# Transposes of the early blocks' exponentials: from the scores' banks into the bank of the small products

## Chip, cores and metric

The kernel runs on one core of a Trainium2 chip. The metric is the device time of one execution in microseconds; a lower time is better. The engines are named as in the profile: PE is the matrix engine (PEld its weight loads, PEldq and PEq its queue), DVE the vector engine, ACT the scalar engine, POOL GpSimd, SP the queue that starts most transfers.

## What is computed

Three parts follow each other: attention over a window of 128 positions with a bias that falls with distance, a dense layer pair, and a mixture of eight experts of which each token uses one. The shapes are 4 batches, 8 heads, 576 positions, 64 numbers a head, so 2304 tokens of 512 numbers.

```python
scores = q @ k.T / sqrt(64);  scores = where(0 <= i - j < 128, scores + bias, -1e9)
x = softmax(scores) @ v                       # attention, to (2304, 512)
h = x @ w_in;  x = (h - tanh(h)) @ w_out      # 512 -> 2048 -> 512
e = argmax(norm(x) @ norm(emb).T / tau)       # one expert of 8 a token
out = gate * (relu(x @ w1[e]) @ w2[e])        # 512 -> 1024 -> 512
```

## The kernel before

The 2304 tokens are 18 blocks of 128. A block's attention is cut into four quarters of two heads each, `jj` 0 and 1 (`quarter`, called with `a = 4 * b + ...`). The first four blocks (`early`, `b < 4`, quarters 0 to 15) take another way than the rest: their scores are made from float32 q and k (L456), and their exponentials are turned by TensorE, where the later blocks write them as two float16 halves and have a transfer turn them (L513).

One early quarter is this chain, for `jj` 0 and 1 each: `scores` on PE (L456, 128 queries by 128 keys for the first block, by 256 for the others); `soft` on DVE (L484), which adds the bias in place and takes the row extreme; `exp` on ACT (L498) into the SBUF tile `p32`, which has two places that quarters use in turn; `tr_pe` on PE (L518), one transpose of 128x128 for each 128 keys; `tr_out` on ACT or DVE (L524), the copy of the turned exponentials into `pt`; and then, for both heads, `pv_f` on PE (L535), the product with the values. After every second quarter DVE divides by the sums (L553, L554, L572), and after a whole block `x_out` turns the block's 512 columns on PE (L633) and splits them into a high and a low part (L645 on ACT, L646 on DVE).

PSUM has eight banks of 2 KiB a partition. Two of them belong to the scores, one for each `jj`. Before the change each holds a tile of 512 float32 numbers a partition in two halves, the scores in half 0 and the turned exponentials in half 1:

```python
self.scores = [self.psA.tile([128, 2, 2, 128], F32, ...) for n in range(2)]
sc = self.scores[jj][:, 0]      # scores()
t = self.scores[jj][:, 1]       # tr_pe(), tr_out()
```

The waits between engines are placed from the tiles that instructions touch, in the order in which the instructions are issued. One more bank, `misc` (`Builder.misc`), serves the small products in turn: the turned embedding of the experts (L269), the turned blocks of `x_out`, and later those of the routing. Its content is held from the product to the last read of it.

The order of all instructions on all engines is made by a list scheduler (`Plan`). Each step is added with its engines and their assumed costs, a due time, and the keys that it reads and writes; `take="misc"` and `free="misc"` mark the first and the last user of the shared bank, and a step that takes it isn't placed while another holds it. Of the steps that are ready, `Plan.order` places the one that can start first, at equal starts the one with the lower due time, and where a step may go to several engines the one that ends it first. Each engine then works strictly in that order. An early quarter's due times rise by half a unit a quarter.

At the same time as the early blocks, the weights `w_in` and `w_out`, which arrive as 64-bit integers, are turned into pairs of float32 parts on ACT (L307, L313, L325), DVE (L309, L313, L328, L331) and POOL or DVE (L317). The dense layer pair starts between the quarters as soon as its first weights and blocks are ready (L686 into the bank `h`, L691 to L703 between, L710 into `acc`).

Of the kernel before, what the change touches and what calls it, by code (L numbers as in the profile page):

```python
# [10 lines left out]
F32 = mybir.dt.float32  # L11
# [151 lines left out]
class Builder:  # L163
# [15 lines left out]
    def setup(self):  # L179
        nc, i = self.nc, self.i  # L180
        self.cst = self.pool("cst", bufs=1)
        self.rt = self.pool("rt", bufs=1)
        self.m1 = self.pool("m1", bufs=2)
        self.xTs = [self.m1.tile([128, XR, KD, 128], F32R, name=f"xT{n}", bufs=1) for n in range(2)]
        self.wp = self.pool("wp", bufs=1)
        self.at = self.pool("at", bufs=2, side="right")
        self.psA = self.pool("psA", bufs=1, space=PSUM)

        self.con = self.cst.tile([128, 129 + E + E + NB], F32, name="con")
        c = iter(np.cumsum([0, 128, E, E, NB, 1]).tolist())  # L190
        c0 = next(c)
        cut = []
        for c1 in c:
            cut.append(self.con[:, c0:c1])
            c0 = c1
        self.ident, self.em8, self.ebase, self.tokid, self.tau = cut
        self.tri = self.cst.tile([128, 128], BF16, name="tri")
        self.ones = self.cst.tile([128, 128], BF16, name="ones")
        self.half = self.cst.tile([128, 1], F32, name="half")
        self.NOV = (NT - CAP + 127) // 128  # L200
        self.thr = self.cst.tile([1, E, self.NOV], F32, name="thr")
        self.cnt = self.cst.tile([128, E], F32, name="cnt")
        self.big = self.cst.tile([128, E], F32, name="big")
        self.cap = self.cst.tile([128, E], F32, name="cap")
        self.gap = self.cst.tile([128, E], F32, name="gap")
        self.ids = self.cst.tile([1, 3 * E], I32, name="ids")
        self.nt = self.cst.tile([1, 2 * E + 1], I32, name="nt")
        self.enT = self.cst.tile([128, KD, E], F32, name="enT")
        self.wst = self.rt.tile([128, 2 * ROW], F32, tag="x2row", name="wst", bufs=1)
        self.wf = [self.wst[:, 0:512], self.wst[:, 512:1024], self.rt.tile([128, 512], F32, tag="xt", name="wst2", bufs=1)]  # L210
        self.wf += [self.at.tile([128, 512], F32, name=f"wf{n}", bufs=1) for n in range(NWF - 3)]
        self.bias = self.at.tile([128, H, 2 * 128], BF16, name="bias", bufs=1)
        self.khl = self.at.tile([128, 2, H, 128], F32R, name="khl", bufs=1)
        self.vt = self.at.tile([128, 2, H, 3 * D], BF16, name="vt", bufs=1)
        self.scores = [self.psA.tile([128, 2, 2, 128], F32, tag=f"sc{n}", name=f"sc{n}") for n in range(2)]
        self.cum = self.rt.tile([128, E], BF16, name="cum")
        self.oh = self.rt.tile([128, 2, E], BF16, name="oh")

# [217 lines left out]
    def quarter(self, P, a, due):  # L436

        nc = self.nc
        b, qd = divmod(a, 4)
        hf, qq = divmod(qd, 2)  # L440
        s, n = b % 2, (2 * b + hf) % 2
        one = b in NOPRE
        W = 128 if one else 256
        v = {"sc": [None, None], "mx": [None, None]}
        pb = a % 2 if a < NPX else 0
# [2 lines left out]
        sk = (a // 2) % 2  # L448

        def scores(jj):  # L450
            sc = v["sc"][jj] = self.scores[jj][:, 0]
            j = qq + 2 * jj
            hp, p0 = hf * 4 + j, 64 * jj
            if early:
                x = slice(1, 2) if one else slice(0, 2)
                nc.tensor.matmul(sc[:, 0:W // 128, :], lhsT=self.qf[b // 2][p0:p0 + 64, b % 2, hf * 2 + qq, :],  # L456
                                 rhs=self.kf[max(b, 1)][p0:p0 + 64, x, hf * 2 + qq, :], start=True, stop=True)
                return
            q = self.qst[n]
            sl = s if one else slice(0, 2)  # L460
            for m in range(2):
                nc.tensor.matmul(sc[:, sl, :], lhsT=q[:, m, j, :], rhs=self.khl[:, sl, hp, :], start=(m == 0),  # L462
                                 stop=(m == 1))
# [48 lines left out]
            v["pt"] = self.at.tile([128, 8, 128], F16, tag=f"pt{a % 2}", name="pt", bufs=1)  # L512
            nc.sync.dma_start_transpose(out=v["pt"][:, 0:4 * W // 128, :], in_=v["ph"][:, 0:4 * W])  # L513

        def tr_pe(jj):
            t = self.scores[jj][:, 1]
            for x in range(W // 128):
                nc.tensor.transpose(t[:, x, :], v["p32"][:, jj * W + x * 128:jj * W + (x + 1) * 128], self.ident)  # L518

        def tr_out(e, jj):  # L520
            if jj == 0:
                v["pt"] = self.at.tile([128, 512], F32, tag=f"pt{a % 2}", name="ptf", bufs=1)
            t = self.scores[jj][:, 1].rearrange("p s t -> p (s t)")
            (nc.scalar.copy if e == "ACT" else nc.vector.tensor_copy)(  # L524
                out=v["pt"][:, jj * W:(jj + 1) * W], in_=t[:, 0:W])

        def pv_f(e):
            KB = W // 128
# [52 lines left out]
        for jj in range(2):  # L581
            if early:
                P.add({"PE": 0.45 if one else 0.65}, lambda e, jj=jj: scores(jj), due,
                      r=["at", ("qf", b)] + [("kf", max(b, 1), x) for x in ([1] if one else [0, 1])], w=[("sc", jj)])
            else:
                P.add({"PE": 0.11 if one else 0.22}, lambda e, jj=jj: scores(jj), due,
                      r=["at"] + ks + [("kl", x, hf) for x in kv] + q, w=[("sc", jj)])
        for jj in range(2):
            P.add({"DVE": ttr}, lambda e, jj=jj: soft(jj), due, r=["at", ("bias", qd * 2 + jj)],
                  w=[("sc", jj), ("mx", jj, a % 2)])  # L590
        for jj in range(2):
            P.add({"ACT": 0.57 if one else 0.67}, lambda e, jj=jj: exp(jj), due,
                  r=["at", ("sc", jj), ("mx", jj, a % 2)], w=[("p32", pb, jj), ("sm", sk, qq, jj)])
        sm = [("sm", sk, x, y) for x in range(2) for y in range(2)]
        half = [("xr", 2 * hf), ("xr", 2 * hf + 1)]
        if early:
            for jj in range(2):
                P.add({"PE": 0.28 if one else 0.5}, lambda e, jj=jj: tr_pe(jj), due, r=["at", "con", ("p32", pb, jj)],
                      w=[("tp", jj)])
            for jj in range(2):  # L600
                P.add({"ACT": 0.3, "DVE": 0.29} if one else {"ACT": 0.38, "DVE": 0.42}, lambda e, jj=jj: tr_out(e, jj),
                      due, r=["at", ("tp", jj)], w=[("pt", a % 2, 1)] if jj else [("pt", a % 2), ("pt", a % 2, 1)])
            P.add({"PE": 0.85 if one else 1.65}, pv_f, due,
                  r=["at", ("pt", a % 2), ("pt", a % 2, 1)] + [("vf", x) for x in ([b] if one else [b - 1, b])], w=[("o", qq)] if qq else ["o", ("o", 0), ("o", 1)])
            if qq:
                P.add({"DVE": 0.5}, recip, due, r=["at"], w=sm)
                P.add({"DVE": 0.4}, mul, due, r=["at", "o", ("o", 0), ("o", 1)] + sm, w=half if hf else [("xr", m) for m in range(4)])
            return
        P.add({"ACT": 0.25, "DVE": 0.2} if one else {"ACT": 0.47, "DVE": 0.34}, s_hi, due, r=["at", ("p32", pb, 0), ("p32", pb, 1)],
              w=[("ph", a % 2)])  # L610
        P.add({"POOL": 0.6, "DVE": 0.33} if one else {"POOL": 1.02, "DVE": 0.6}, s_lo, due,
              r=["at", ("p32", pb, 0), ("p32", pb, 1), ("ph", a % 2)], w=[("ph", a % 2, 1)])
        P.add({"SP": 0.5 if one else 0.9}, tr, due, r=["at", ("ph", a % 2), ("ph", a % 2, 1)], w=[("pt", a % 2)])
        P.add({"PE": 0.27 if one else 0.53}, pv, due,
              r=["at", ("pt", a % 2)] + [("vt", x, hf, m) for x in kv for m in range(3)], w=["o"])
# [802 lines left out]
```

## Time and profile before

| what | value |
|---|---|
| time, median of 3 runs (lowest to highest) | 847.39 us (847.25 to 847.75) |
| the profiled execution: time / span of its instructions | 849.56 us / 847.8 us |
| PE busy / weight loads busy, share of the span | 96% / 85% |
| DVE, ACT, POOL busy, share of the span | 67%, 52%, 30% |
| the early quarters' transposes (L518) on PE | 56, first at 7.3 us, last at 84.5 us |
| their copies (L524) | 32: 26 on ACT, 6 on DVE |

The span runs from the first to the last instruction of the profiled execution. A busy share is a mean over stages that have different limits. Before about 143 us the kernel prepares weights and the early blocks; after that PE runs nearly without a break to the end.

### The profile page before, as it was taken

How to read it: one execution, taken by the hardware profiler on the slowest of the kernel's cores; microseconds unless marked ns; L12 is line 12 of the kernel's file. 1: busy time of each engine (PE TensorE's matmuls, PEld its weight loads, DVE VectorE, ACT ScalarE, POOL GpSimd, SP SyncE). 2: the span in 40 equal slices, each digit the busy share in tenths (PEclk: the TensorE clock that was granted, in tenths of full speed). 3: DMA queues.
4: the chain of work that ended last, by engine and by line, in shares of the span. 5: the costliest groups of instructions: out<-in, count | busy, mean ns of one | idle time of the engine just before them, and what ended most of it. 6: DMA issues, size and time to landing. Idle time of an engine off the chain costs nothing.

```text
span 847.8 us, 15246 instructions
## 1 busy us (share of the span) xinstructions
PE 816.7 (96%) x5244; PEld 721.2 (85%) x5244; DVE 565.5 (67%) x1500; ACT 441.6 (52%) x997; POOL 252.1 (30%) x246
## 2 busy tenths in 40 slices
PE   6999999999999999999999999999999999999995
PEld 4677878988888899988998998989889899998994
DVE  4658999987778577777776775576366656666230
ACT  3759876665555355555554543464255545545120
POOL 1424676554424233324242240021110210111011
PEclk9999999999999999999999999999999999999998
DMA  8973325945334234433434312365266656555000
GB/s 299 334 268 121 109 94 160 270 107 130 96 82 135 40 82 106 87 87 91 99 83 102 80 41 48 125 212 162 84 198 216 216 166 189 193 163 174 20 27 30
DMA packets 109464, 112.88 MB, mean 133 GB/s; under 512 B 62901, under 2 KB 75189, under 8 KB 109248
## 3 DMA queue, kind: packets, MB, share of 16 engines
q1 hardware_dynamic: 106240, 102.35, 42.2%
q0 software_dynamic: 3136, 9.46, 3.0%
q8 instruction: 43, 0.70, 0.4%
q14 instruction: 45, 0.37, 0.1%
HBM read 87.12 MB, written 17.48 MB: 123 GB/s over the span
## 4 chain that ended last, share of the span: by engine, by line
PE 71%; DVE 11%; DMA 7%; issue 6%; ACT 2%; SPq 2%; POOL 1%; POOLq 0%; DVEq 0%; ACTq 0%
PE h L686 19%; PE acc L710 17%; PE he L1014 9%; PE y L1049 8%; PE o L546 3%; DMA pt<-ph 3%; PE sc L456 3%; PE sc L462 2%; DMA out<-yo,ix 2%; DVE wst L331 2%; PE y L1045 2%; PE misc L785 2%; PE of L535 2%; DVE rawo L328 1%; PE sc L518 1%
## 5 line engine op out<-in xcount | busy, mean ns | idle before, releaser
L686 PE MATMUL h<-xT,wi 128*128 128x256 f32 x1728 | 228.8, 287 | 0.0
L686 PEld LDWEIGHTS h<-xT,wi 128*128 128x128 f32 x1728 | 219.4, 193 | 6.4 <-issue 2.6
L710 PE MATMUL acc<-wo,gh 128*128 128x512 f32 x576 | 183.9, 400 | 0.0
L710 PE MATMUL acc<-wo,gl 128*128 128x512 f32 x288 | 112.9, 392 | 2.0 <-DVE gl L703 2.0
L710 PEld LDWEIGHTS acc<-wo,gh 128*128 128x128 f32 x576 | 99.7, 189 | 15.1 <-issue 0.7
L691 ACT ACTIVATE t<-h 128x512 f32<-128x512 f32 x72 | 43.1, 599 | 100.3 <-PE h L686 95.3
L1049 PE MATMUL y<-eo,ge 128*128 128x512 f32 x336 | 88.5, 399 | 0.0
L484 DVE CUSTOM_DVE_ANT_0 sc<-sc,bias 128x256 f32<-128x256 f32 (+1 forms) x144 | 52.7, 372 | 46.3 <-PE sc L462 29.4
L498 ACT ACTIVATE p<-sc,mx 128x256 f32<-128x256 f32 (+1 forms) x128 | 59.3, 464 | 34.1 <-DVE mx L484 26.0
L1074 POOL DMA_INDIRECT out<-yo,ix x24 | 23.4, 975 | 176.2 <-PE y L1045 61.0
L1049 PEld LDWEIGHTS y<-eo,ge 128*128 128x128 f32 x336 | 60.0, 188 | 9.7
L710 PEld LDWEIGHTS acc<-wo,gl 128*128 128x128 f32 x288 | 54.1, 188 | 15.1 <-DVE gl L703 2.9
L508 POOL TENSOR_TENSOR ph<-p,ph 128x512 f16<-128x512 f32 (+1 forms) x38 | 46.1, 1214 | 69.3 <-ACT ph L503 26.0
L703 DVE TENSOR_TENSOR gl<-t,gh 128x512 fp32r<-128x512 f32 x72 | 63.0, 876 | 4.6 <-ACT gh L699 4.4
L948 DVE TENSOR_TENSOR eo<-est,eo 128x512 fp32r<-128x512 f32 x60 | 45.0, 752 | 30.4 <-ACT eo L944 29.4
L1036 DVE SCALAR_TENSOR_TENSOR ge<-he,ge 128x256 fp32r<-128x256 f32 x104 | 29.9, 325 | 51.9 <-ACT ge L1030 51.9
L694 DVE TENSOR_TENSOR t<-h,t 128x512 f32<-128x512 f32 x72 | 49.5, 687 | 19.0 <-ACT t L691 19.0
L944 ACT CAST eo<-est 128x512 fp32r<-128x512 f32 x64 | 39.7, 620 | 40.1 <-PE y L1045 21.5
L1014 PE MATMUL he<-xT,ei 128*128 128x320 f32 x384 | 60.4, 309 | 0.0
L1014 PEld LDWEIGHTS he<-xT,ei 128*128 128x128 f32 x384 | 58.3, 188 | 2.3
L1030 ACT ACTIVATE ge<-he 128x320 fp32r<-128x320 f32 (+1 forms) x56 | 24.1, 430 | 67.5 <-PE he L1014 61.7
L1014 PE MATMUL he<-xA,ei 128*128 128x320 f32 (+1 forms) x384 | 59.0, 302 | 0.0
(181 smaller groups left out, 1425.6 us busy)
## 6 DMA issues: line engine op xcount, KB each, us to landing
est<-in_w SPq DMA_DIRECT2D x128, 256.0 KB, 2.9
rawi<-in_w_in SPq DMA_DIRECT2D x16, 512.0 KB, 6.6
rawo<-in_w_out SPq DMA_DIRECT2D x16, 512.0 KB, 7.3
stk<-in_k SPq DMA_DIRECT2D x30, 256.0 KB, 2.7
stq<-in_q SPq DMA_DIRECT2D x28, 256.0 KB, 2.8
bucket<-in_c_pad SPq DMA_DIRECT2D x8, 771.0 KB, 5.8
xe<-bucket SPq DMA_DIRECT2D x17, 257.0 KB, 3.5
vst<-in_v SPq DMA_DIRECT2D x30, 128.0 KB, 2.4
```

Of the source, the lines that this page charges most:

```text
L484: nc.vector.tensor_tensor_reduce(out=x, in0=x, in1=self.bias[:, h, c0:c1], scale=-0.125, scalar=mx[:, 1:2] if m else 3.0e38, op0=ALU.add, ...
L498: nc.scalar.activation(out=v["p32"][:, jj * W:(jj + 1) * W], in_=x, func=AF.Exp, scale=-1.0, bias=v["mx"][jj][:, 0:1], accum_out=self.sums ...
L508: self.eng(e).tensor_tensor(out=ph[:, 2 * W:4 * W], in0=v["p32"][:, 0:2 * W], in1=ph[:, 0:2 * W], op=ALU.subtract)
L686: nc.tensor.matmul(h3(v["h"], f2), lhsT=w[:, a, k, :], rhs=xT[c][:, :, k, :], start=(k == 0 and n == 0), stop=(k == KD - 1 and n == 2))
L691: nc.scalar.activation(out=v["t"], in_=v["h"].rearrange("p a b -> p (a b)"), func=AF.Tanh)
L694: nc.vector.tensor_tensor(out=v["t"], in0=v["h"].rearrange("p a b -> p (a b)"), in1=v["t"], op=ALU.subtract)
L703: self.eng(e).tensor_tensor(out=v["gl"], in0=v["t"], in1=v["gh"].bitcast(F32), op=ALU.subtract)
L710: nc.tensor.matmul(self.acc[g, t], lhsT=v[a][:, c0:c0 + 128], rhs=self.w["o", fs[f2]][:, c, :], start=(first and f2 == 0 and n == 0), stop ...
L944: nc.scalar.copy(out=t[:, 0, :], in_=v["x"])
L948: self.eng(eng).tensor_tensor(out=t[:, 1, :], in0=v["x"], in1=t[:, 0, :].bitcast(F32), op=ALU.subtract)
L1014: nc.tensor.matmul(h[:, 0:N], lhsT=w[:, a, c0:c0 + 128], rhs=xT()[b][:, k, 0:N], start=(k == 0 and n == 0), stop=(k == KD - 1 and n == 2))
L1049: nc.tensor.matmul(y[t], lhsT=gt(f, a)[:, (t - ts[0]) * 128:(t - ts[0] + 1) * 128], rhs=self.w["o", f0 + f][:, b, :], start=(f == 0 and n ...
```

## The change

In the early quarters the transposes of both heads go into one tile from the shared bank `misc`: four of 128x128 (two in the first block) are issued in one step, and one copy of 512 columns (256 in the first block) takes them out, where before each head had its own transposes in the second half of its scores' bank and its own copy. The tiles of the scores keep only the scores. For the scheduler the two transposing steps (0.5 each, 0.28 in the first block) become one (1.0, 0.6) that needs both heads' exponentials and takes `misc`; the two copies (0.38 on ACT or 0.42 on DVE) become one (0.6 or 0.69) that frees `misc`.

```diff
--- before.py
+++ after.py
@@ -212,7 +212,7 @@
         self.bias = self.at.tile([128, H, 2 * 128], BF16, name="bias", bufs=1)
         self.khl = self.at.tile([128, 2, H, 128], F32R, name="khl", bufs=1)
         self.vt = self.at.tile([128, 2, H, 3 * D], BF16, name="vt", bufs=1)
-        self.scores = [self.psA.tile([128, 2, 2, 128], F32, tag=f"sc{n}", name=f"sc{n}") for n in range(2)]
+        self.scores = [self.psA.tile([128, 2, 128], F32, tag=f"sc{n}", name=f"sc{n}") for n in range(2)]
         self.cum = self.rt.tile([128, E], BF16, name="cum")
         self.oh = self.rt.tile([128, 2, E], BF16, name="oh")
 
@@ -448,7 +448,7 @@
         sk = (a // 2) % 2
 
         def scores(jj):
-            sc = v["sc"][jj] = self.scores[jj][:, 0]
+            sc = v["sc"][jj] = self.scores[jj]
             j = qq + 2 * jj
             hp, p0 = hf * 4 + j, 64 * jj
             if early:
@@ -512,17 +512,15 @@
             v["pt"] = self.at.tile([128, 8, 128], F16, tag=f"pt{a % 2}", name="pt", bufs=1)
             nc.sync.dma_start_transpose(out=v["pt"][:, 0:4 * W // 128, :], in_=v["ph"][:, 0:4 * W])
 
-        def tr_pe(jj):
-            t = self.scores[jj][:, 1]
-            for x in range(W // 128):
-                nc.tensor.transpose(t[:, x, :], v["p32"][:, jj * W + x * 128:jj * W + (x + 1) * 128], self.ident)
-
-        def tr_out(e, jj):
-            if jj == 0:
-                v["pt"] = self.at.tile([128, 512], F32, tag=f"pt{a % 2}", name="ptf", bufs=1)
-            t = self.scores[jj][:, 1].rearrange("p s t -> p (s t)")
-            (nc.scalar.copy if e == "ACT" else nc.vector.tensor_copy)(
-                out=v["pt"][:, jj * W:(jj + 1) * W], in_=t[:, 0:W])
+        def tr_pe(e):
+            v["tp"] = self.misc()
+            for x in range(2 * W // 128):
+                c = slice(x * 128, (x + 1) * 128)
+                nc.tensor.transpose(v["tp"][:, c], v["p32"][:, c], self.ident)
+
+        def tr_out(e):
+            v["pt"] = self.at.tile([128, 512], F32, tag=f"pt{a % 2}", name="ptf", bufs=1)
+            (nc.scalar.copy if e == "ACT" else nc.vector.tensor_copy)(out=v["pt"][:, 0:2 * W], in_=v["tp"][:, 0:2 * W])
 
         def pv_f(e):
             KB = W // 128
@@ -594,14 +592,12 @@
         sm = [("sm", sk, x, y) for x in range(2) for y in range(2)]
         half = [("xr", 2 * hf), ("xr", 2 * hf + 1)]
         if early:
-            for jj in range(2):
-                P.add({"PE": 0.28 if one else 0.5}, lambda e, jj=jj: tr_pe(jj), due, r=["at", "con", ("p32", pb, jj)],
-                      w=[("tp", jj)])
-            for jj in range(2):
-                P.add({"ACT": 0.3, "DVE": 0.29} if one else {"ACT": 0.38, "DVE": 0.42}, lambda e, jj=jj: tr_out(e, jj),
-                      due, r=["at", ("tp", jj)], w=[("pt", a % 2, 1)] if jj else [("pt", a % 2), ("pt", a % 2, 1)])
+            P.add({"PE": 0.6 if one else 1.0}, tr_pe, due, r=["at", "con", ("p32", pb, 0), ("p32", pb, 1)], w=[("tp", a)],
+                  take="misc")
+            P.add({"ACT": 0.4, "DVE": 0.42} if one else {"ACT": 0.6, "DVE": 0.69}, tr_out, due, r=["at", ("tp", a)],
+                  w=[("pt", a % 2)], free="misc")
             P.add({"PE": 0.85 if one else 1.65}, pv_f, due,
-                  r=["at", ("pt", a % 2), ("pt", a % 2, 1)] + [("vf", x) for x in ([b] if one else [b - 1, b])], w=[("o", qq)] if qq else ["o", ("o", 0), ("o", 1)])
+                  r=["at", ("pt", a % 2)] + [("vf", x) for x in ([b] if one else [b - 1, b])], w=[("o", qq)] if qq else ["o", ("o", 0), ("o", 1)])
             if qq:
                 P.add({"DVE": 0.5}, recip, due, r=["at"], w=sm)
                 P.add({"DVE": 0.4}, mul, due, r=["at", "o", ("o", 0), ("o", 1)] + sm, w=half if hf else [("xr", m) for m in range(4)])
```

## Rows read from the trace of the kernel before

**Rows 1.** The page, part 1: busy time of PE and of its weight loads.
```profile
PE 816.7 (96%) x5244; PEld 721.2 (85%) x5244; DVE 565.5 (67%) x1500; ACT 441.6 (52%) x997; POOL 252.1 (30%) x246
```

**Rows 2.** Stretches: length, busy time and instructions by engine, granted clock, DMA share, GB/s.
```profile
10.00:66.00 56.00, 55.00 (x189) 39.45 (x188) 33.14 (x95) 34.90 (x96) 15.37 (x14) 1.00 0.89 314
66.00:100.00 34.00, 30.90 (x200) 24.97 (x200) 31.88 (x56) 29.47 (x67) 19.18 (x12) 1.00 0.37 119
100.00:143.00 43.00, 39.88 (x256) 35.28 (x256) 42.14 (x55) 31.83 (x62) 32.50 (x23) 1.00 0.30 93
```

**Rows 3.** Waits of the first 100 us: total us, times, longest us.
```profile
ACT ptf L524 <- PE sc L456: 16.1, 14, 2.5
...
DVE sc L484 <- ACT ptf L524: 13.3, 14, 2.4
...
PE sc L518 <- ACT p L498: 2.0, 4, 1.0
...
PE misc L633 <- DVE xr L572: 1.7, 1, 1.7
```

**Rows 4.** Order of time, 0 to 60 us: start us, us, engine, line, operation [idle before].
```profile
20.35 0.27 ACT L524 COPY ptf<-sc 128x128 f32<-128x128 f32 x1 [0.67 <-PE sc L456]
...
20.65 0.43 DVE L484 CUSTOM_DVE_ANT_0 sc<-sc,bias 128x256 f32<-128x256 f32 x1 [1.01 <-ACT ptf L524]
...
21.69 0.69 PE L518 MATMUL sc<-con,p 128*128 128x128 f32 x2 [0.33 <-ACT p L498]
...
28.82 1.23 PE L456 MATMUL sc<-kf,qf 64*128 64x256 f32 x4
```

**Rows 5.** Order of time, 30 to 56 us.
```profile
30.63 1.97 PE L535 MATMUL of<-vf,ptf 128*128 128x64 f32 x8 [0.58 <-DVE ptf L524]
...
38.78 1.80 PE L456 MATMUL sc<-kf,qf 64*128 64x256 f32 x4
...
44.46 1.06 PE L633 MATMUL misc<-con,xr 128*128 128x128 f32 x4
...
47.99 0.68 DVE L646 TENSOR_TENSOR xT<-misc,xT 128x512 fp32r<-128x512 f32 x1
...
48.36 0.63 PE L518 MATMUL sc<-con,p32x 128*128 128x128 f32 x2
...
50.08 2.93 PE L686 MATMUL h<-xT,wi 128*128 128x256 f32 x12
```

**Rows 6.** The chain that ended last, 0 to 160 us: start us, us, engine, line.
```profile
28.04 0.85 PE sc L518 x4
...
32.60 0.43 PE sc L518 x2
33.02 1.15 PE sc L456 x2
34.17 0.62 PE sc L518 x2
```

**Rows 7.** Order of time, 55 to 130 us.
```profile
62.31 2.93 PE L686 MATMUL h<-xT,wi 128*128 128x256 f32 x12
...
66.88 0.70 PE L456 MATMUL sc<-kf,qf 64*128 64x256 f32 x4
...
67.51 1.71 PE L686 MATMUL h<-xT,wi 128*128 128x256 f32 x12
...
68.02 0.43 DVE L484 CUSTOM_DVE_ANT_0 sc<-sc,bias 128x256 f32<-128x256 f32 x1 [1.40 <-ACT ptf L524]
...
70.80 0.44 PE L518 MATMUL sc<-con,p 128*128 128x128 f32 x2 [0.51 <-ACT p L498]
```

**Rows 8.** Copies out of the transposes: count, ns minimum/median/maximum, first and last start.
```profile
L524 ACT COPY ptf<-sc x26: 266/372/390, 10.2 to 86.3; 128x256 f32<-128x256 f32 x22, 128x128 f32<-128x128 f32 x4
L524 DVE COPY ptf<-sc x6: 289/292/425, 9.5 to 46.7; 128x128 f32<-128x128 f32 x4, 128x256 f32<-128x256 f32 x2
```

**Rows 9.** A 128x512 copy out of a bank, order of time, 80 to 112 us.
```profile
105.06 1.06 ACT L662 COPY xspill<-acc 128x512 f32<-128x512 f32 x2
```

## Prediction

> **What bounds the kernel now.** I read the page first: PE is busy 96% of the span [rows 1], so only two things can move the end: the PE work itself, and the 31 us in which PE has nothing to do. The table of stretches then says where the edited steps live. Between 10 and 66 us PE is busy 55.00 of 56.00 us, DVE 33.14 and ACT 34.90: PE is the limit there, and ACT and DVE have over 20 us of slack each [rows 2]. From 66 to 100 us DVE fills 31.88 of 34.00 and PE 30.90, from 100 to 143 us DVE 42.14 of 43.00 and PE 39.88: there DVE, at work on the weights, sets the pace and PE has 6.2 us of idle time [rows 2]. The last early transposes come at 84.5 us, so nothing that is edited runs later.
>
> The table of waits comes next. In the first 100 us ACT stood 16.1 us in front of the copy of the transposes, put down to the score product L456, and DVE stood 13.3 us in front of the bias step L484, put down to that copy [rows 3]. Neither needs the other's data. The copy needs L518, which was done earlier; but the next quarter's scores go into the other half of the same tile, so the copy waits until they are written, and the bias step of those scores then waits for the copy. One case in order of time: the copy starts at 20.35, after 0.67 us of waiting for L456; the bias step follows at 20.65, 1.01 us idle; and the transposes at 21.69 come after 0.33 us of PE idle time for the exponentials [rows 4]. Of all this waiting only what reaches PE can count where PE is the limit, and PE's own total for the exponentials in 100 us is 2.0 us [rows 3].
>
> **The change part by part.** *Transposes.* Their number stays at 56. In the chain four in a run take 0.85 us; two take 0.43 after another kind of product, 0.62 right after a score product [rows 6]. A quarter whose heads were apart pays 0.43 + 0.62 = 1.05; one run of four behind a score product would pay 0.85 + (0.62 - 0.43) = 1.04. That is 0. If all ten apart quarters got their run elsewhere it would be 10 x 0.20 = -2.0; the upper end is 0, since a run can't be split any more.
>
> *Score products.* The two heads lie on different 64 rows of the array. Issued next to each other both take 1.23 us [rows 4], issued apart 1.15 each [rows 6], 2.30 in all: a pair saves 1.1 us (0.70 for a pair once PE is quick [rows 7]). Six of the sixteen quarters are paired now. The scheduler pairs them when both exponentials of the quarter before are done as PE comes free, else it puts the transposes between. After the change a lone first head can't be transposed, so the score of head 0 goes first, then the four transposes (lower due time), then head 1: still apart. I take 0, with one or two pairs more or fewer, -2.2 to +2.2.
>
> *Waits that go.* The score tile is free of the copy, so four PE stalls lose their cause: 0.58 before L535 at 30.63 and the 0.57 by which the pair at 38.78 is longer than the one at 28.82 (1.80 - 1.23) [rows 4, 5], 0.33 at 21.69 [rows 4], 0.51 at 70.80 [rows 7]. Sum -2.0. Bounds: 0 (the next wait in the same place takes over) and -2.5 (with more hidden in the modelled ends, as at 38.78).
>
> *DVE's entry into its full stretch.* At 68.02 DVE is idle 1.40 us for the copy [rows 7]; from there on it has next to no slack. What it gains there reaches PE only at waits such as the 1.7 us of L633 for DVE [rows 3]. Between 0 and -1.4 I take -0.7, the middle, because PE is nearly as full as DVE in that stretch [rows 2].
>
> *Copies.* 32 become 16. On ACT a 256-column copy takes 372 ns [rows 8], a 512-column one 1.06 / 2 = 0.53 [rows 9]: 2 x 0.372 - 0.53 = 0.21 us of ACT a quarter. It is hidden by ACT's slack up to 66 us; without that cover it would be 12 x 0.21 = -2.6. Should the scheduler send copies to DVE after 66 us, each would cost the full stretch about 0.7 (the 512-column read of a bank at 47.99 took 0.68 [rows 5]); six of the 32 went there before, all before 47 us [rows 8]. 0.
>
> *Longer waits.* All four transposes now wait for head 1's exponentials; the score of head 0 (1.15) stands in front and covers it. L535 waits for a copy of 0.53 in place of two of 0.37, covered by the score of head 1 (1.15) [rows 6]; where ACT is late L535 is what stands, with PE behind it, up to 0.5 a time. 0.
>
> *The shared bank.* New is that the transposes queue with `x_out` for it. `x_out` of block 1 starts its products at 44.46 and its last reader ends at 47.99 + 0.68 = 48.67; the next transposes ran at 48.36 [rows 5]. They would wait 0.3 us, and behind them on PE the scores, L535 and L686. Three such crossings lie before the last early quarter: +0.9 at 0.3 each. Bounds: 0, if other products fill the time, and 48.67 - 45.52 = 3.15 each, +9.4, if transposes stand right behind all three. I stay near the low end since the scheduler knows that the bank is held and places other products.
>
> Sum: -2.0 - 0.7 + 0.9 = -1.8 us, so 849.56 - 1.8 = 847.8 for the profiled execution, and 847.39 - 1.8 = 845.6 for the median, which lies 2.2 below the profiled one.
>
> **The clock of PE.** [...] Yet twelve matmuls of L686 take 2.93 us in each of the three bursts from 50.08 to 62.31 and 1.71 in the one at 67.51 [rows 5, 7], and a pair of scores 1.23 and then 0.70 [rows 4, 7]. So PE ran at little over half speed until about 66 us, and what it did before it became quick was the third burst of dense matmuls; the stretch of scores and transposes before had not done it. A change in the order of these bursts moves that moment. [...] No row here separates transposes from scores in this, so I leave it out of the sum and make it two rivals.
>
> **The rivals.** *Nothing to measure* (0.22). The four stalls come back as others, since in 56 us PE has 1.0 us of idle time all told [rows 2]: 847.2.
>
> *PE becomes quick a burst or two earlier* (0.20). For: one burst in three did it, and freed DVE and ACT work lets bursts move together. Against: bursts start by due time, as before. Right after the first (53.0 in place of 66.0) it is worth 13.0 x (1 - 1.71 / 2.93) = 5.4 us, halfway 2.7: 845.6 less that, 840.2 to 842.9.
>
> *PE becomes quick later* (0.12). For: the third burst stood next to scores, and two at 50.08 didn't suffice alone. If the burst of 67.51 is needed too, the 3.6 us from 66.9 to 70.5 take 2.93 / 1.71 as long, +2.6; if 10 us more pass, +7.1, part of it hidden by DVE: 848.2 to 852.5.
>
> *The shared bank stalls PE: slower* (0.12). Transposes that stand right behind `x_out` wait 3.15 us on PE with everything after them. It decides from the second full wait: -2.7 + 2 x 3.15 = +3.6, 851.0; one is +0.5, 847.9. For: DVE is idle in other places and late at L646. Against: at 44.46 the gap to the next transposes was 3 us already [rows 5].
>
> **How the numbers follow.** The forecast, 845.6, has 0.34, with its own range 843.6 to 847.2 from the bounds of the stalls and one pair. About 0.2% (1.7 us) is what a measurement of this kernel can tell from no change. Faster by more: 0.24 of the forecast and the 0.20 of the early clock, 0.44. Within: 0.10 of the forecast, 0.22 of nothing, 0.02 of the bank: 0.34. Slower: 0.10 of the bank, 0.12 of the late clock: 0.22. The range 841.0 to 851.0 leaves out the earliest clock (0.08) and the tails of the two slow cases (0.11).
>
> **What would show it.** Right: in the profile after, no wait of L524 for L456 and none of L484 for L524; L518 in runs of four; PE busy in the stretch 10 to 66 the same or a little shorter; the first quick L686 near 64 to 66 us. Wrong: L518 or L633 waiting for L524, L645 or L646 by whole microseconds; more or fewer L456 in pairs; the 2.93 us bursts ending at another count than three; copies on DVE after 66 us.

## Result and the profile after

The changed kernel takes 838.67 us (median of 4 runs, 838.14 to 839.09), the kernel before 847.57 (4 runs). The ratio is 0.9907, 95% interval 0.9885 to 0.9929: 8 to 9 us faster, where 1.8 was forecast, and below the stated range. The profiled execution took 838.14 us, so nothing has to be taken off between its span and the median. Two lines of its page, against [rows 1]:

```profile
span 836.4 us, 15221 instructions
...
PE 799.7 (96%) x5244; PEld 709.6 (85%) x5244; DVE 569.1 (68%) x1502; ACT 438.5 (52%) x985; POOL 248.1 (30%) x240
```

PE has 17 us less busy time for the same 5244 matmuls, and still 37 us of idle time, more than the 31 before: the gain isn't idle time that was closed. The stretches, columns as in [rows 2]:

```profile
10.00:66.00 56.00, 49.80 (x275) 36.94 (x275) 49.20 (x119) 49.15 (x125) 22.11 (x17) 0.97 0.92 329
66.00:100.00 34.00, 31.17 (x208) 27.41 (x207) 32.29 (x41) 27.27 (x53) 25.14 (x16) 1.00 0.33 110
100.00:143.00 43.00, 36.05 (x241) 31.16 (x241) 39.13 (x87) 28.74 (x65) 30.29 (x23) 1.00 0.57 162
```

The first line is the result. Up to 66 us PE issues 275 matmuls in place of 189, in 49.80 us of busy time in place of 55.00, and DVE and ACT get through 49 us of work each in place of 33 and 35. The second line has changed little; in the third PE is 3.8 us less busy and the transfers move more. How much earlier the whole is shows in the matmuls of the first dense layer (L686, L682 after the change; length, PE busy and count, clock, DMA), first before, then after:

```profile
0.00:107.00 107.00, 22.46 (x139) 1.00 0.66 226
0.00:119.00 119.00, 28.67 (x188) 1.00 0.60 207
```

```profile
0.00:107.00 107.00, 26.11 (x192) 0.98 0.68 235
```

The kernel before has issued 188 of them at 119 us, the changed one 192 at 107: 12 us by then. The two profiled times differ by 849.56 - 838.14 = 11.4. The lead is complete much earlier: the second burst of twelve starts at 57.88 in the kernel before and at 46.44 in the changed one (the last line of PE's order of time below), which is 11.4 us already. So all of it arises in the part with the early blocks.

```profile
57.88 2.93 PE L686 MATMUL h<-xT,wi 128*128 128x256 f32 x12
```

The waits of the first 100 us, to be held against [rows 3]:

```profile
DVE sc L484 <- PE sc L456: 4.7, 6, 1.5
...
PE misc L629 <- ACT ptf L523: 1.7, 2, 0.9
PE of L533 <- ACT ptf L523: 1.6, 4, 0.6
PE misc L519 <- ACT p32x L498: 1.5, 2, 1.3
PE sc L456 <- ACT p L498: 1.4, 2, 0.9
PE sc L456 <- ACT p32x L498: 1.3, 3, 0.6
...
ACT ptf L523 <- PE misc L519: 1.0, 2, 0.7
```

The 16.1 us of copies behind scores and the 13.3 us of bias steps behind copies are gone, as forecast. PE now waits for the one copy, L533 for 1.6 us and `x_out` (L629) for 1.7 us for its turn in the shared bank, and for the exponentials, L519 for 1.5 us and the scores for 1.4 and 1.3. All 16 copies run on ACT, a 512-column one in 575 ns:

```profile
L523 ACT COPY ptf<-misc x16: 358/575/600, 10.1 to 73.8; 128x512 f32<-128x512 f32 x12, 128x256 f32<-128x256 f32 x4
```

And PE's own order of time (start, us, line):

```profile
15.86 1.23 PE L456 MATMUL sc<-kf,qf 64*128 64x256 f32 x4
...
21.53 1.23 PE L456 MATMUL sc<-kf,qf 64*128 64x256 f32 x4
...
23.55 1.00 PE L533 MATMUL of<-vf,ptf 128*128 128x64 f32 x8
...
42.05 2.52 PE L682 MATMUL h<-xT,wi 128*128 128x256 f32 x12
...
46.44 1.67 PE L682 MATMUL h<-xT,wi 128*128 128x256 f32 x12
```

Of the sixteen pairs of score products ten are now issued next to each other (x4), against six. PE runs at double pace from about 23 us, not 66: a product with the values takes 1.00 us for eight matmuls at 23.55, where it took 1.97 at 30.63 before [rows 5]. It falls back once, from about 39 to 44 us (granted clock 0.82 from 38 to 42 and 0.75 from 42 to 46): the burst at 42.05 takes 2.52, the next 1.67.

So four things differ at once: the waits, the pairs, the order, and the moment at which PE becomes quick. The runs below take them apart.

### The profile page after: what moved, and what is told of

Its sections match the earlier page's. It is cut to its first block, busy times and chain, and to the rows that moved or that the text cites. A ratio compares the mean times of both kernels' runs of the same rounds, so it can differ in the third digit from the quotient of the medians.

```text
span 836.4 us, 15221 instructions
## 1 busy us (share of the span) xinstructions
PE 799.7 (96%) x5244; PEld 709.6 (85%) x5244; DVE 569.1 (68%) x1502; ACT 438.5 (52%) x985; POOL 248.1 (30%) x240
## 4 chain that ended last, share of the span: by engine, by line
PE 74%; DVE 8%; DMA 8%; issue 3%; ACT 2%; SPq 2%; POOL 1%; POOLq 0%; DVEq 0%
PE h L682 19%; PE acc L706 18%; PE he L1010 12%; PE y L1045 10%; PE o L544 4%; DMA pt<-ph 3%; PE y L1041 3%; PE sc L462 3%; DVE wst L331 2%; DMA stk<-in_k 2%; PE misc L781 2%; DMA out<-yo,ix 1%; DVE rawo L328 1%; PE misc L968 1%; SPq L915 1%
## 5 line engine op out<-in xcount | busy, mean ns | idle before, releaser
L682 PE MATMUL h<-xT,wi 128*128 128x256 f32 x1728 | 226.2, 286 | 0.0
L682 PEld LDWEIGHTS h<-xT,wi 128*128 128x128 f32 x1728 | 218.4, 192 | 5.5 <-issue 1.0
L1010 PEld LDWEIGHTS he<-xA,ei 128*128 128x128 f32 x384 | 56.3, 188 | 2.6
```

Of the source, the lines that this page charges most:

```text
L682: nc.tensor.matmul(h3(v["h"], f2), lhsT=w[:, a, k, :], rhs=xT[c][:, :, k, :], start=(k == 0 and n == 0), stop=(k == KD - 1 and n == 2))
L1010: nc.tensor.matmul(h[:, 0:N], lhsT=w[:, a, c0:c0 + 128], rhs=xT()[b][:, k, 0:N], start=(k == 0 and n == 0), stop=(k == KD - 1 and n == 2))
```

## Experiments

Every kernel was timed in three rounds beside the kernel before on the same chip. The ratio to that is what is compared; medians are in us. The executions of some kernels spread widely, those of e4 from 840.70 to 846.94 and those of e7 from 839.22 to 848.22, so that the sizes of their gains are loose.

| run | median | kernel before | ratio (95% interval) |
|---|---|---|---|
| e1 before, dense start | 851.35 | 846.97 | 1.0049 (1.0021 to 1.0077) |
| e2 after, dense start | 842.97 | 846.97 | 0.9964 (0.9936 to 0.9992) |
| e3 order of after, banks of before | 852.07 | 846.97 | 1.0058 (1.0036 to 1.0080) |
| e4 order of before, banks freed | 844.21 | 846.97 | 0.9967 (0.9947 to 0.9987) |
| e5 after, again | 839.94 | 846.95 | 0.9916 (0.9890 to 0.9942) |
| e6 before, all pairs | 845.57 | 846.95 | 0.9981 (0.9966 to 0.9995) |
| e7 before, dense quarters | 842.26 | 846.95 | 0.9963 (0.9932 to 0.9993) |
| e8 after, dense quarters | 840.13 | 846.95 | 0.9920 (0.9889 to 0.9951) |
| e9 banks freed, dense quarters | 840.74 | 847.69 | 0.9932 (0.9902 to 0.9961) |
| e10 banks freed, all pairs | 838.98 | 847.69 | 0.9908 (0.9874 to 0.9943) |
| e11 after, two copies | 840.54 | 847.69 | 0.9928 (0.9903 to 0.9954) |
| e12 after, all pairs | 847.17 | 847.69 | 0.9997 (0.9980 to 1.0013) |

**The first theory: PE is quick earlier, and that is the gain** (theory A). Four runs were set against it and theory B, that the waits between the halves of a bank were the cost. e1 and e2 keep PE at work while it waits for the first transfer:

```diff
+            one = self.vt[:, 0, 0:3, :].rearrange("p h d -> p (h d)")
+            nc.vector.memset(one, 1.0)
+            w = self.misc("acc1")
+            for m in range(11):
+                nc.tensor.matmul(w, lhsT=one[:, 0:128], rhs=one[:, 0:512], start=True, stop=True)
             for fn, e in P.order({"misc": 1}):
```

> The kernel before, with 11 matmuls of 512 columns on a tile of ones while PE waits for the first transfer (0.9 to some 5.5 us); their product is not used. Theory A (the change wins because PE becomes quick 43 us earlier): if PE is quick from 6 us on, the twelve-matmul bursts take 1.7 us from the first one and the time falls by 6 us or more, to 841 or less. If it becomes quick but falls back before 20 us, little changes and A stays untested. Theory B (the change wins because the copies and bias steps no longer wait for each other's bank): PE is quick early, but the time stays within 2 us of 847.5, since ACT and DVE still stand in the old waits.

> The changed kernel, with the same 11 matmuls at the start. Theory A: PE is quick some 15 us earlier still, worth at most half of that: 838.7 less 1 to 5, 834 to 838. Theory B: no change, 838 to 839.5. If PE falls back to slow before 20 us, both say 838 to 840.

Neither held PE at the quick level in the early stage (e2 reads a granted clock of 0.51 from 10 to 24 us and 0.60 from 24 to 40). The eleven matmuls of e1, then e1 in stretches, columns as in [rows 2], and last the kernel before from 40 to 66 us:

```profile
1.65 4.88 PE L1236 MATMUL misc<-vt 128*128 128x512 bf16 x11 [1.65 <-DVE vt L1233]
```

```profile
10.00:24.00 14.00, 13.36 (x42) 8.94 (x43) 7.59 (x30) 8.01 (x25) 2.73 (x3) 0.54 1.04 356
24.00:40.00 16.00, 15.33 (x54) 10.46 (x52) 9.89 (x28) 11.45 (x31) 6.47 (x6) 0.50 1.05 362
40.00:66.00 26.00, 26.00 (x97) 20.04 (x97) 16.18 (x40) 15.69 (x40) 6.39 (x7) 0.51 0.73 264
```

```profile
40.00:66.00 26.00, 26.00 (x96) 19.82 (x94) 16.11 (x40) 15.46 (x40) 6.37 (x7) 1.00 0.73 265
```

The granted clock is 0.54 and then 0.50 and 0.51 up to 66 us. The runs therefore decide nothing on A; the eleven matmuls also put the first scores at 6.46 us, a microsecond later (5.46 in the kernel before), and e1 is 4 us slower, e2 behind the other runs of the changed kernel (842.97) and above all that was expected of it. But they settle one thing. This kernel's PE work in these stretches is that of the kernel before nearly matmul for matmul (97 in 26.00 us against 96 in 26.00 from 40 to 66 us), and here the trace records the clock: the early stage of the kernel before has the pace that goes with 0.50 to 0.54 in e1, though its own profile shows 1.00 there [rows 2].

**Order against banks.** e3 has the steps and the order of the changed kernel, but the transposes go back into the scores' banks:

```diff
-            v["tp"] = self.misc()
             for x in range(2 * W // 128):
-                c = slice(x * 128, (x + 1) * 128)
-                nc.tensor.transpose(v["tp"][:, c], v["p32"][:, c], self.ident)
+                jj, k = divmod(x, W // 128)
+                nc.tensor.transpose(self.scores[jj][:, 1, k, :], v["p32"][:, x * 128:(x + 1) * 128], self.ident)
...
+            for jj in range(2):
+                t = self.scores[jj][:, 1].rearrange("p s t -> p (s t)")
...
+                    out=v["pt"][:, jj * W:(jj + 1) * W], in_=t[:, 0:W])
```

> The order and the steps of the changed kernel, but the transposes go into the second halves of the scores' banks and come out in two copies, so that the waits between the halves are back. Theory A: PE issues the same products in the same order, becomes quick at about the same time (within 3 us of 23 us), and the time stays at 838 to 841. Theory B: the waits of the copies for the scores are back, 16 us of them on ACT, and the time returns to 845 to 848.

e4 is the opposite: order and steps of before, transposes of blocks 0 to 2 in the two banks that the second dense product needs only later:

```diff
-            t = self.scores[jj][:, 1]
+            if b < 3:
+                v["tp", jj] = self.misc(f"acc{jj}")[:, 0:256].rearrange("p (s t) -> p s t", s=2)
+            else:
+                v["tp", jj] = self.scores[jj][:, 1]
+            t = v["tp", jj]
```

> The order and the steps of the kernel before, but the transposes of blocks 0 to 2 go into the two banks that the second product of the dense layers uses only later, so that copies and scores no longer share a bank up to some 66 us. Theory A: the order of PE's products is the old one, PE becomes quick at 62 to 66 us as before and the time falls by the 1 to 2 us of the PE stalls alone, to 845.5 to 847. Theory B: the waits are gone and with them most of the 9 us: 838 to 842.

With the old banks the new order is not better but slower than the kernel before, 1.0058, and above what either theory expected. PE becomes quick only at about 56 us (eight matmuls with the values take 1.81 us at 49.56 and 1.10 at 57.24), so theory A's condition, 23 us, wasn't met. The waits are back, and the scores themselves now stand behind copies for 2.1 us. Only eight pairs of scores are left with no wait between the two heads, and two of these take 2.33 us, as much as two apart (waits, then the stretch, then PE):

```profile
DVE sc L484 <- ACT ptf L524: 8.5, 10, 2.2
ACT ptf L524 <- PE sc L456: 8.0, 9, 2.0
...
PE sc L456 <- ACT ptf L524: 2.1, 3, 1.0
```

```profile
10.00:66.00 56.00, 51.75 (x210) 37.42 (x209) 37.21 (x99) 39.41 (x112) 15.21 (x13) 1.00 0.90 317
```

```profile
25.90 2.33 PE L456 MATMUL sc<-kf,qf 64*128 64x256 f32 x4
...
57.24 1.10 PE L535 MATMUL of<-vf,ptf 128*128 128x64 f32 x8
```

From e3 to the changed kernel only the banks and the number of copies differ, and e11 below shows that the copies cost nothing measurable: in this order the free banks are worth the step from 1.0058 to 0.9907.

With the banks freed in the old order the gain is 0.33%, between what A and B expected. The stretch of e4 and one of its products with the values:

```profile
10.00:66.00 56.00, 55.33 (x233) 39.57 (x234) 41.69 (x106) 40.80 (x110) 18.54 (x15) 1.00 0.95 332
```

```profile
52.41 1.00 PE L539 MATMUL of<-vf,ptf 128*128 128x64 f32 x8
```

PE is full there, 55.33 of 56 us, as in the kernel before, but with 233 matmuls in place of 189. It is quick from about 51 us (twelve dense matmuls take 2.93 us at 48.40 and 1.71 at 53.97) and not, as expected, from 62 to 66, so a part of its gain may be the clock.

**Does the moment matter?** The changed kernel was run again, unaltered.

> The changed kernel once more, unaltered, to be timed on the same chip as the runs below and for a second profile. Theory A (the moment at which PE becomes quick decides the time): where this profile shows another moment than 23 us, its time differs from 838.7 by some 0.3 us for each us of moment or more. Theory C (with the waits gone ACT and DVE set the pace early on, and the moment counts little): 838 to 842 wherever the moment lies.

```profile
10.00:24.00 14.00, 14.00 (x53) 9.93 (x54) 9.56 (x31) 9.93 (x30) 3.69 (x3) 1.00 1.07 377
24.00:40.00 16.00, 15.60 (x70) 11.59 (x70) 15.22 (x36) 15.31 (x39) 8.34 (x8) 0.61 1.04 360
40.00:66.00 26.00, 24.70 (x153) 19.88 (x152) 24.07 (x55) 23.62 (x57) 9.41 (x8) 0.91 0.77 286
```

This execution, too, becomes quick near 23 us, but then shows PE at a granted clock of 0.50 from 28 to 44 us, 0.61 and 0.91 being means over the stretches. In finer ones, and with the second burst of the dense layer:

```profile
24.00:28.00 4.00, 3.60 (x21) 2.53 (x20) 3.97 (x11) 4.00 (x12) 2.21 (x3) 0.95 1.02 323
28.00:36.00 8.00, 8.00 (x34) 6.04 (x35) 7.39 (x21) 7.67 (x19) 3.44 (x4) 0.50 1.04 368
36.00:44.00 8.00, 8.00 (x35) 6.25 (x35) 7.64 (x20) 6.99 (x19) 3.22 (x2) 0.50 1.07 380
44.00:48.00 4.00, 4.00 (x29) 3.54 (x29) 2.64 (x6) 3.45 (x10) 2.52 (x2) 0.91 1.03 406
```

```profile
47.41 1.67 PE L682 MATMUL h<-xT,wi 128*128 128x256 f32 x12
```

The profiled execution took 839.07 us; the one that was quick for most of the time from 23 us on took 838.14. More than 10 us more at half clock go with 1 us, where theory A asked for 5 or more. DVE still gets through 48.85 us of work from 10 to 66 us, as before in 49.20. The second burst starts 10.5 us ahead of that of the kernel before (57.88), which is the whole difference between the two profiled times (849.56 - 839.07), after a stretch in which PE was mostly slow. Theory A falls for the changed kernel: its gain is there without a PE that stays quick from 23 us. No run keeps it slow up to 66 us, as the kernel before is; what the quick level adds between 45 and 66 us isn't separated, but the lead at the end is no larger than at that burst.

**Pairs, and a quick PE, in the kernel before.** e6 makes the two score products of a quarter one step:

```diff
-        for jj in range(2):
-            if early:
-                P.add({"PE": 0.45 if one else 0.65}, lambda e, jj=jj: scores(jj), due, ..., w=[("sc", jj)])
+        if early:
+            P.add({"PE": 0.9 if one else 1.3}, lambda e: [scores(jj) for jj in range(2)], due, ...,
+                  w=[("sc", 0), ("sc", 1)])
```

> The kernel before with one edit: the score products of both heads are one step of the scheduler (its cost is the sum), so that all sixteen pairs are issued next to each other; transposes, copies and banks are the old ones. If the pairs (10 in place of 6 in the changed kernel) are what won, ten more pairs at 1.1 us while PE is slow give 5 to 9 us: 838 to 842. If the waits between copies and scores are what held the kernel back, they stay: 845 to 850.

e7 (and e8, the same on the changed kernel) puts dense work in front of each product with the values:

```diff
         def pv_f(e):
+            if a < 11:
+                w = self.misc("acc1")
+                for m in range(5):
+                    nc.tensor.matmul(w, lhsT=self.bias[:, 0, 0:128], rhs=self.bias[:, 0:2, :], start=True, stop=True)
```

> The kernel before with 5 matmuls of 512 columns, unused, in front of each product with the values in quarters 0 to 10, to make PE quick early. Theory A: PE is quick from some 15 to 20 us, and the time falls below 843 although the dummies cost up to 12 us of PE. Theory C: PE may be quick, but the copies still wait for scores and the bias steps for copies; the time stays at 845 or rises.

> The changed kernel with the same dummies. Theory A: PE is quick from some 15 us to the end, and the time falls by 1 to 4 us under that of the changed kernel on the same chip. Theory C: PE is quick, but the time stays within 1.5 us of that of the changed kernel, or rises by what the dummies put in front of real products.

All pairs give 0.19% in the old banks, and the copies still stand 8.6 us behind scores. The wait, and then the stretch, where PE is busy only 47.71 of 56 us:

```profile
ACT ptf L524 <- PE sc L456: 8.6, 8, 2.3
```

```profile
10.00:66.00 56.00, 47.71 (x224) 34.89 (x222) 44.02 (x107) 44.06 (x118) 21.86 (x17) 1.00 0.92 321
```

e7 was quick from 15 us on, as the five added matmuls (L531) show in PE's order of time (start, us), and gained 0.37% (ratio 0.9963, down to 0.9932) in spite of 55 added matmuls. Its bursts, then its stretch:

```profile
11.39 2.31 PE L531 MATMUL misc<-bias 128*128 128x512 bf16 x5
...
15.34 1.24 PE L531 MATMUL misc<-bias 128*128 128x512 bf16 x5
```

```profile
10.00:66.00 56.00, 54.45 (x310) 36.97 (x310) 43.47 (x114) 43.81 (x119) 21.44 (x16) 1.00 0.92 329
```

So in the kernel before the slow PE did cost. In the changed kernel the same dummies, with PE quick from 16 us (four matmuls with the values take 0.55 us at 16.45, 0.96 at 12.97), give 840.13, the time of e5 within the intervals.

**Both levers in the old order** (theory D: a slow PE and the shared banks paced the old stage together). e9 frees the banks for the first ten quarters and adds the dummies of e7; e10 frees them for the first eleven (its expectation says ten) and makes all pairs, as e6. Transposes and copies stay by head.

```diff
-            t = self.scores[jj][:, 1]
+            if a < 10:
+                v["tp", jj] = self.misc(["acc0", "h1"][jj])[:, 0:256].rearrange("p (s t) -> p s t", s=2)
+            else:
+                v["tp", jj] = self.scores[jj][:, 1]
+            t = v["tp", jj]
```

```diff
-            t = self.scores[jj][:, 1]
+            if a < 11:
+                v["tp", jj] = self.misc(f"acc{jj}")[:, 0:256].rearrange("p (s t) -> p s t", s=2)
+            else:
+                v["tp", jj] = self.scores[jj][:, 1]
+            t = v["tp", jj]
```

> The kernel before, its order and its steps, with both levers at once: the transposes of quarters 0 to 9 in banks that nothing else uses yet, and 5 unused dense matmuls in front of the products with the values of quarters 0 to 10. Theory D (the old stage was paced by a slow PE in a ring with the shared banks; either lever loosens it, and behind it ACT, DVE and the transfers set one floor): some 165 matmuls of L686 in the first 100 us as in the changed kernel, and 838 to 841. Theory P (the changed kernel's order with its ten pairs is needed too): no better than with either lever alone, 842 to 845.

> The kernel before with all pairs of scores in one step (as in e6) and the transposes of quarters 0 to 9 in unused banks, transposes and copies still by head. Theory D: PE is relieved by the pairs, the waits are gone, so the floor is reached: 838 to 841. Theory W (the waits alone matter): as e4, 843 to 845. If the single step for both heads' transposes is what counts: 845.

The stretch of e9, then that of e10, one of its products with the values and its first two dense bursts:

```profile
10.00:66.00 56.00, 55.41 (x322) 38.09 (x321) 45.55 (x119) 45.08 (x123) 20.86 (x16) 1.00 0.93 329
```

```profile
10.00:66.00 56.00, 51.77 (x252) 38.39 (x249) 50.04 (x116) 48.28 (x128) 24.69 (x18) 1.00 0.93 327
```

```profile
39.15 1.97 PE L539 MATMUL of<-vf,ptf 128*128 128x64 f32 x8
...
45.98 2.91 PE L693 MATMUL h<-xT,wi 128*128 128x256 f32 x12
...
50.38 1.70 PE L693 MATMUL h<-xT,wi 128*128 128x256 f32 x12
```

Both reach the changed kernel within the intervals: 0.9932 and 0.9908. The interval of e9 also overlaps those of e4 and e7; that of e10 lies below those of e4 and e6. e10 has neither the one step nor the one copy nor the shared bank, and only banks and pairs in common with the changed kernel. Its PE is slow up to some 48 us (1.97 for eight matmuls at 39.15, 2.91 for the first dense burst), and its second burst starts 7.5 us ahead of that of the kernel before, with one more product with the values still to come (1.00 us at 51.91), so most of its gain, too, isn't a quick PE.

**Parts of the change.** e11 cuts the copy in two, e12 makes all sixteen pairs.

```diff
+            for c in (slice(0, W), slice(W, 2 * W)):
-                ...(out=v["pt"][:, 0:2 * W], in_=v["tp"][:, 0:2 * W])
+                ...(out=v["pt"][:, c], in_=v["tp"][:, c])
```

> The changed kernel with its copy cut in two of 256 columns, one after the other in the same step. The order is the same, ACT has some 0.2 us more a quarter. Theory D: ACT is near the floor early on, so 0 to 2 us slower than the changed kernel, 839 to 841. If the single copy is a main part of the gain: 842 or more.

> The changed kernel with the scores of both heads in one step of the scheduler, so that all sixteen quarters are paired in place of ten. Theory D: PE no longer paces the stage, so within 1.5 us of the changed kernel, 838 to 841. Theory P: 2 to 5 us less, 834 to 837, and then this is the fastest version.

Two copies cost nothing that the intervals show. e12 fell against both theories: forced pairs take the whole gain away, 0.9997. Its PE waits (then its stretch) are of another kind:

```profile
PE of L533 <- ACT ptf L523: 5.5, 6, 2.1
PE misc L519 <- ACT p32x L498: 4.7, 3, 2.0
```

```profile
10.00:66.00 56.00, 45.35 (x200) 32.62 (x199) 49.57 (x108) 46.23 (x113) 25.02 (x19) 1.00 0.90 321
```

PE is idle 10.65 of 56 us. My reading, which no run isolates, is that the score of head 0 can no longer fill the time in which PE waits for the second exponentials or for the single copy. In e10, with a bank, a step and a copy for each head, the same pairs are the good version; which of the three makes the difference isn't shown. e12 also shows that a busy DVE is no gain by itself: 49.57 us there and 50.04 in e10, but 200 matmuls against 252.

## Why the prediction was wrong

**The step that failed** is the one in the first part: "Of all this waiting only what reaches PE can count where PE is the limit", with PE busy 55.00 of 56.00 us as its ground. A busy row is no measure of how much work PE gets done. From 28 to 44 us the kernel before and e5, an execution of the changed one, both have PE at its slow level (eight matmuls with the values take 1.97 us in both) and nearly full. The kernel before there, to be held against the two middle lines of e5 above:

```profile
28.00:36.00 8.00, 7.42 (x26) 4.38 (x24) 4.18 (x14) 5.18 (x15) 2.57 (x3) 1.00 1.06 374
36.00:44.00 8.00, 7.91 (x29) 5.77 (x29) 6.75 (x15) 5.88 (x17) 4.65 (x5) 1.00 0.70 246
```

In 16.00 us of busy time in place of 15.33 the changed kernel issues 69 matmuls, not 55 (some four of the 69 belong to the dense burst that starts at 43.23), and DVE and ACT do about a third more work (15.03 and 14.66 us in place of 10.93 and 11.06). In these lines nearly the same busy time holds different amounts of work. I had quoted the prices of paired and unpaired scores and still took the sum of busy time as fixed.

**What holds in its place.** The early stage was a ring through a slow PE and shared banks. Pairs alone: -1.4 us (845.57 - 846.95), and PE then stands idle, so the waits limit. Banks alone: -2.8 (844.21 - 846.97), and PE stays full, so PE limits. Both: -8.7 (838.98 - 847.69), and then DVE is busy 50.04 of 56 us, as in the changed kernel, which does both in one edit (ten pairs of the sixteen). By the medians that is more than the sum of the two; as ratios it is 0.92% with 0.57 to 1.26 against 0.19 and 0.33% with some 0.15 to 0.2 on either side, so that a plain sum isn't excluded. What is shown is that each lever is worth something alone and that the two together (e10) are worth as much as the change. In the changed kernel itself the banks are shown to be needed (e3); what its four further pairs are worth there was not run apart.

Its steps in turn:

- *Transposes, 0; copies, 0.* Right for the copies: e11 shows no price of the second copy, and no copy went to DVE. The price of the 56 transposes was not separated.
- *Score products, 0.* Wrong. "Still apart" was the step: ten of sixteen were paired, four more than before. The bounds, one or two pairs, were too near. The price of 1.1 us was not too low: ten more pairs in free banks, e10 against e4, are 0.9908 against 0.9967, 5.0 us or 0.5 a pair, and in the old banks (e6) 1.4 us for all ten. Four pairs more at 1.1 us would have moved the forecast to 841.2.
- *Waits that go, -2.0.* About right for the banks alone in the old order (-2.8 in e4, 0.9947 to 0.9987), but mis-sized for the change: with the pairs it is 8.7 (e10), and in the new order the banks are worth the step from e3 to the changed kernel.
- *DVE's entry, -0.7.* Mis-sized: I priced the 1.40 us at 68.02. DVE had done 16 us more work by 66 us, which no single idle gap showed. How much of that reaches the end isn't shown: e12 has as much of it and no gain.
- *Longer waits, 0.* Too low: PE waits 1.6 us before L533 and 1.5 before L519.
- *The shared bank, +0.9.* It stalls PE, but from the other side: `x_out` waits 1.7 us for the transposes' copy. The two waits are longer than the 0.3 us priced, and the time fell all the same.
- *Rival "PE becomes quick earlier".* It happened, at 23 us, and staying quick from there isn't the cause: e5 has the time with PE slow again from 28 to 44 us. The level between 45 and 66 us stays unseparated, as said above. In the old ring an early quick PE is worth 0.37% (e7, 0.07 to 0.68%), some 3 us; the rival had priced it at 2.7 to 5.4.
- *Rival "nothing to measure".* Refuted by the time, although stalls did come back as others: PE's idle time between 10 and 66 us rose from 1.0 to 6.2 us.
- *Rivals "PE becomes quick later" and "the shared bank stalls PE: slower".* Neither happened.

Open: why e3 is slower than the kernel before; its scores wait for copies, which breaks up pairs, and two of the pairs that are left gain nothing, but no run took its one step of transposes apart from the banks. And why PE, lifted near 23 us in both profiled executions of the changed kernel, fell back at about 39 us in one and at 28 in the other; in both it is quick again from about 45.

## What to carry to other kernels

An engine at 98% busy need not be a fixed limit: PE issued 189 matmuls in 55.00 us of busy time before and 275 in 49.80 after. So compare counts of instructions in the stretch, and look for the same instruction at two prices (here 1.97 and 1.00 us for eight matmuls with the values), before waits of other engines are called free. More busy time on the other engines is no proof of progress either: DVE was busy 49.57 us in e12, at 847.17, and 50.04 in e10, at 838.98. Where two steps of one ring share a PSUM bank only to save space, look at the wait for the other half of the tile as part of the ring: here 16.1 us of copies behind scores, and 0.33% for the freed banks alone (e4). And when two limits lie in one ring, time both removals together before either is written off as small: here 0.19% (e6), 0.33% (e4) and 0.92% for both (e10).

## What the hardware showed

The profile of the kernel before reads a granted clock of 1.00 up to 66 us, but from 40 to 66 us its PE issues 96 matmuls in 26.00 us where e1 issues 97, and e1 reads 0.51 there (0.54 from 10 to 24 us, 0.50 from 24 to 40). In e1, with 4.88 us of dense matmuls from 1.65 us on, two score matmuls of the first block take 0.49 us at 8.45 (0.79 at 7.70 in the kernel before), but four with the values take 1.11 at 10.98, as at 11.20 in the kernel before: PE wasn't quick for long. With five dense matmuls in front of every product with the values it was quick from 15 us (e7: the five take 2.31 us at 11.39 and 1.24 at 15.34). The same program was quick from 23 to 39 us in one execution (1.00 us for eight matmuls with the values at 23.55 and at 38.25, 2.52 for the dense burst at 42.05) and from 23 to 28 in the next (1.97 for the eight at 30.78), and in both from about 45 to 143 us (1.10 for the eight at 45.13 and 46.11, granted clock 1.00 from 66 to 143; after, e5).
